# Attention and two MLPs on one core: an early first exponential, other decoding steps for the second MLP, state-row sums over 64 columns

## The chip, the core and the metric

The kernel runs on one core of a Trainium2 chip. The metric is the device time of one execution in microseconds (us); the median of several runs is compared. The engines have these names in profiles: PE (TensorE's matmuls), PEld (its weight loads, which overlap the matmuls), DVE (VectorE), ACT (ScalarE), POOL (GpSimd) and SP (SyncE, which issues most DMAs).

## What is computed

Cross attention between 8 x 8 heads' 512 tokens and 32 state rows, in both directions, then two MLPs over all 8 x (512 + 32) = 4352 rows of 512 features. All data are float32.

```python
scores = x @ state.T / sqrt(64)              # 512 x 32 per head
xread = softmax(scores) @ state              # 512 x 64
scores2 = state @ x.T / sqrt(64)             # 32 x 512
sread = softmax(scores2) @ x                 # 32 x 64: the state rows' sums over tokens
y = concat(xread, sread), heads side by side # (8 * 544) x 512
h = y @ w_in1;  g = h * sigmoid(1.702 * h);  y = g @ w_out1
h = y @ w_in2;  g = h * cos(h);              out = g @ w_out2
```

The inner width is 2048. The softmax subtracts the maximum and adds 1e-9 to the sum.

## The kernel before

**Tiles and steps.** Tokens are cut into nine tiles: t = 0 to 7 are the 512 tokens of one batch each, and t = 8 (the tail) holds all batches' 256 state rows, collected in `xs`. A step (m, t, c) handles MLP m, tile t and 128 of the 2048 inner columns, so a tile has 16 steps c. MLP 1 takes the tiles in the order 0 to 6, tail, 7; MLP 2 takes 0 to 3, tail, 4 to 7. In a step PE does `hidden` (the product with w_in, into `ph`), then `second` of two steps earlier (the product with w_out, added up in `py0` to `py3`, which have one buffer each). Between them lies the activation: `gate` in MLP 1 (tanh L383, multiply L385, high part gh L373, low part gl L375) and `cosine` in MLP 2 (L409 to L420, then `times`).

**Float32 in pieces.** Products are made of three passes of a rounded high part and a low part (`wh`, `wl`, `xh`, `xl`). Weights come packed as 64-bit words and are decoded on the chip, in sixteen units per MLP: eight of w_in and eight of w_out, 1 MB each. `fetch_w` loads a unit, `decode_begin` gives two ScalarE operations (`top` L121, `bottom` L124), and in the next step `decode_end` gives `bits` (VectorE, L137), `hi` (ScalarE, L143) and `lo` (VectorE, L147). `units` says in which step a unit is begun. The second MLP's units are begun at the steps of `at2` (L615), in the order w_in 0 to 7, w_out 0 to 7: four in the tail tile of MLP 1 (steps 6, 9, 12, 15), seven in tile 7 of MLP 1 (2, 4, ... 14) and five in the first tile of MLP 2 (3, 5, 7, 10, 12).

**Order.** The whole order is written by hand (`tc.manual_schedule`): each engine runs its instructions in the order in which the Python code issues them, and so does each queue. Loads of a step stand on SP's queue behind all earlier ones.

**Attention.** `attn_pieces(b, g)` gives the pieces for batch b and half g (four heads). `scores` multiplies four heads at a time, each in its own 32 columns of the array; q counts these heads. `max_n`, `exp_n`, `norm_n`, `xread` are the softmax over state rows and the product with the states; `max_s`, `exp_s`, `norm_s`, `turn_s`, `sread`, `place_s` are the softmax over tokens, a transpose, the sums over tokens and their transposes into `xs`. For batches 1 to 7 xread isn't formed: `sw_piece` multiplies states and w_in once, from `rhi` and `rlo`, the two parts of a pair of batches' states in `rblk`, and stores the products in DRAM; `load_sw` loads them. `split_state` makes rhi and rlo; `load_pair` loads the states of a pair.

In `sread` each of four heads multiplies its 32 weight columns with the 128 columns of its head pair, of which only 64 are its own; `place_s` picks those. There are sixteen such sums, each of four token chunks times four heads, and each matmul shows as two in the trace (two passes).

**The start.** Batch 0 is done before the first step. ScalarE's queue issues the loads of `sblk`, `rblk` and `pair0`, then makes rhi of `pair0`; then follow both halves' softmax, `warm(22)` (22 matmuls on the identity, into a place that nothing reads), `xread` and the decoding of the first unit.

**Output.** `store` copies py to `o` and issues the store. In MLP 2, `o` comes from a pool with two buffers.

```python
pool, tag = (ep, "g") if m == 0 and k >= 2 else (op, "o")
```

## Time and profile before

| | us |
|---|---|
| three runs | 1468.28, 1467.53, 1468.15 |
| their median | 1468.15 |
| the profiled execution | 1467.7 |
| its span, from the first to the last instruction | 1465.9 |
| PE busy | 1446.3 (99%) |
| PEld busy | 1188.5 (81%) |
| DVE busy | 928.1 (63%) |
| ACT busy | 646.9 (44%) |
| POOL busy | 112.9 (8%) |

Times in rows are counted from the start of the span. A matmul's busy time overlaps that of the next, so PE's pace is read from starts, not from durations. In a row of a timeline, the bracket gives how long the engine was idle just before, and what ended that; instructions of one line that follow one another are merged (x count). "L366" is line 366 of the kernel. Where an instruction waits for several things, the profile names the one that came last by its own records.

### The profile page before, as it was taken

The page shows a single profiled execution, that of the slowest core. Times are in us where ns is not written, and L with a number is a line of the kernel's source. Part 1 is how long each engine was busy: PE and PEld are TensorE (multiplying, and loading weights), DVE is VectorE, ACT ScalarE, POOL GpSimd, SP SyncE. Part 2 cuts the span into 40 slices and gives each one's busy share as a digit, 9 for nine tenths or more (in the row PEclk, how much of TensorE's full clock was granted, in tenths as well). Part 3 has the DMA queues.
Part 4 walks back from the last instruction along what each step waited for, and adds up shares of the span by engine and source line. Part 5 has one row for each costly group of instructions (what it writes and reads, how often), then busy time and mean ns, then how long its engine had stood idle before and what let it go on. Part 6 is the DMA issues. An engine that isn't in the chain of part 4 may idle for free.

```text
span 1465.9 us, 19331 instructions
## 1 busy us (share of the span) xinstructions
PE 1446.3 (99%) x7310; PEld 1188.5 (81%) x7310; DVE 928.1 (63%) x1641; ACT 646.9 (44%) x1078; POOL 112.9 (8%) x156
## 2 busy tenths in 40 slices
PE   8999999999999999999999999999999999999998
PEld 5878888888887888998877888888888888888886
DVE  6875655565555655456687666666677666666664
ACT  5864344434334343466555333333343343333433
POOL 0111011101010000100000010100000000101000
PEclk9999999999999999999999999999999999999999
DMA  9756565655655353564400101010011000010000
GB/s 341 224 178 195 140 187 140 177 158 144 175 133 166 99 145 108 180 191 169 144 1 0 58 1 58 1 44 0 1 59 44 1 32 26 0 58 1 29 1 29
DMA packets 81340, 140.58 MB, mean 96 GB/s; under 512 B 11616, under 2 KB 38368, under 8 KB 81248
## 3 DMA queue, kind: packets, MB, share of 16 engines
q1 hardware_dynamic: 70944, 109.34, 23.6%
q0 software_dynamic: 8960, 29.37, 8.1%
q8 instruction: 57, 0.93, 0.3%
q10 hardware_dynamic: 1344, 0.66, 0.2%
q14 instruction: 35, 0.29, 0.1%
HBM read 92.14 MB, written 47.19 MB: 95 GB/s over the span
## 4 chain that ended last, share of the span: by engine, by line
PE 88%; DVE 7%; ACT 3%; issue 1%; DMA 1%; POOL 0%; ACTq 0%; DVEq 0%
PE py L452 46%; PE ph L366 26%; PE ph L359 11%; PE psS L176 3%; PE psA L235 1%; PE psC L319 1%; DVE u L137 1%; DVE r L413 1%; DVE r L418 1%; DVE d L417 1%; DVE wo L147 1%; ACT wo L143 1%; PE psB L310 1%; DVE gl L375 1%; ACT rawo L124 0%
## 5 line engine op out<-in xcount | busy, mean ns | idle before, releaser
L366 PE MATMUL ph<-xh,wi 128*128 128x512 f32 (+1 forms) x1280 | 404.6, 379 | 0.0
L452 PE MATMUL py<-gh,wo 128*128 128x512 f32 (+1 forms) x1152 | 362.6, 378 | 2.4 <-ACT wo L143 1.2
L452 PE MATMUL py<-wo,gh 128*128 128x512 f32 x1088 | 335.5, 390 | 0.2 <-ACT gh L373 0.2
L366 PEld LDWEIGHTS ph<-xh,wi 128*128 128x128 f32 x1280 | 237.8, 188 | 49.2 <-DVE xl L287 1.3
L452 PEld LDWEIGHTS py<-gh,wo 128*128 128x128 f32 x1152 | 213.0, 188 | 44.7 <-DVE wo L147 2.0
L366 PE MATMUL ph<-xl,wi 128*128 128x512 f32 (+1 forms) x640 | 241.4, 379 | 0.0
L452 PEld LDWEIGHTS py<-wo,gh 128*128 128x128 f32 x1088 | 203.2, 188 | 41.5 <-ACT gh L373 0.7
L452 PE MATMUL py<-gl,wo 128*128 128x512 f32 (+1 forms) x576 | 217.4, 377 | 0.0
L452 PE MATMUL py<-wo,gl 128*128 128x512 f32 x544 | 212.9, 391 | 4.5 <-DVE gl L375 4.2
L420 ACT ACTIVATE r<-r,half_pi 128x512 f32<-128x512 f32 (+1 forms) x144 | 101.0, 701 | 245.7 <-DVE r L419 245.7
L375 DVE TENSOR_TENSOR gl<-t,gh 128x512 fp32r<-128x512 f32 (+1 forms) x144 | 97.4, 676 | 159.1 <-ACT gh L373 159.1
L373 ACT ACTIVATE gh<-t 128x512 fp32r<-128x512 f32 (+1 forms) x144 | 87.7, 609 | 248.1 <-PE py L452 137.1
L413 DVE TENSOR_SCALAR r<-r 128x512 f32<-128x512 f32 (+1 forms) x144 | 65.5, 455 | 182.4 <-ACT r L409 182.3
L359 PE MATMUL ph<-xh,swt 128*128 128x512 f32 x448 | 160.5, 399 | 0.0
L409 ACT ACTIVATE r<-ph 128x512 f32<-128x512 f32 (+1 forms) x144 | 82.3, 572 | 171.6 <-PE ph L366 171.5
L385 DVE SCALAR_TENSOR_TENSOR t<-t,ph 128x512 f32<-128x512 f32 (+1 forms) x144 | 94.1, 654 | 84.3 <-ACT t L383 84.1
L366 PEld LDWEIGHTS ph<-xl,wi 128*128 128x128 f32 x640 | 120.6, 188 | 22.7
L452 PEld LDWEIGHTS py<-wo,gl 128*128 128x128 f32 x544 | 102.0, 188 | 30.2 <-DVE gl L375 9.2
L452 PEld LDWEIGHTS py<-gl,wo 128*128 128x128 f32 x576 | 108.4, 188 | 20.1
L433 DVE TENSOR_TENSOR r<-r,ph 128x512 f32<-128x512 f32 (+1 forms) x144 | 94.8, 658 | 41.5 <-ACT r L420 41.4
L383 ACT ACTIVATE t<-ph 128x512 f32<-128x512 f32 (+1 forms) x144 | 82.0, 570 | 81.1 <-PE ph L359 65.0
L184 POOL DMA_DIRECT2D sd<-swo x112 | 67.0, 608 | 528.1 <-DVE swo L181 505.9
(78 smaller groups left out, 1505.6 us busy)
## 6 DMA issues: line engine op xcount, KB each, us to landing
sd<-swo POOLq DMA_DIRECT2D x112, 256.0 KB, 3.8
swt<-sd SPq DMA_DIRECT2D x112, 256.0 KB, 4.0
rawi<-in_w_in SPq DMA_DIRECT2D x32, 512.0 KB, 6.5
rawo<-in_w_out SPq DMA_DIRECT2D x32, 512.0 KB, 5.7
xT_t<-in_xT SPq DMA_DIRECT2D x36, 256.0 KB, 4.3
xN_t<-in_xN SPq DMA_DIRECT2D x16, 512.0 KB, 4.2
yd<-o SPq DMA_DIRECT2D x32, 256.0 KB, 2.9
yraw<-yd SPq DMA_DIRECT2D x32, 256.0 KB, 4.4
```

The lines of the kernel that those rows point to most:

```text
L184: nc.gpsimd.dma_start(out=sw_dram[b, f][r0:r0 + D, :, k // 2, :], in_=o[i * D:(i + 1) * D].bitcast(F32).rearrange("p c h f -> p c (h f)"))
L359: nc.tensor.matmul(ph, l, r, start=(g == 0 and i == 0), stop=(g == 1 and i == 2))
L366: nc.tensor.matmul(ph, w[:, f0:f0 + P], x, start=(w is wh and k == 0 and x is xk[0][0]), stop=(w is wl and k == KD - 1))
L373: nc.scalar.activation(out=gh, in_=g, func=AF.Copy)
L375: return lambda: nc.vector.tensor_tensor(out=gl, in0=g, in1=gh.bitcast(F32), op=ALU.subtract)
L383: nc.scalar.activation(out=t1, in_=ph, func=AF.Tanh, scale=0.5 * GATE)
L385: nc.vector.scalar_tensor_tensor(out=g, in0=t1, scalar=1.0, in1=ph, op0=ALU.add, op1=ALU.mult)
L409: nc.scalar.activation(out=r, in_=ph, func=AF.Copy, scale=1.0 / (2.0 * math.pi), bias=0.25)
L413: nc.vector.tensor_scalar(out=r, in0=r, scalar1=MAGIC, scalar2=MAGIC, op0=ALU.add, op1=ALU.subtract)
L420: nc.scalar.activation(out=r, in_=r, func=AF.Sin, bias=half_pi)
L433: nc.vector.tensor_tensor(out=r, in0=r, in1=ph, op=ALU.mult)
L452: nc.tensor.matmul(yt[k], l, r, start=(c == 0 and i == 0), stop=(c == KF - 1 and i == 2))
```

## The change

It has four parts.

1. At the start the first ScalarE instruction is now an exponential of one column (`early`). `pair0` is gone: pair 0 is loaded into `rblk` where pair 1 was, `rhi` and `rlo` of pair 0 are made at step 1 of tile 0 (rlo by POOL), and pair 1 is loaded three steps later. The load of `rblk` moves from ScalarE's queue to SP's. `max_n` is cut into `lay_n` and `most_n`, the pieces of the two halves change their order, and `warm(22)` becomes `warm(16)` before the first xread and `warm(14)` behind it.
2. The second MLP's units are begun at other steps: five in the tail of MLP 1 (6, 8, 10, 12, 14), eight in tile 7 (0, 2, ... 14), three in the first tile of MLP 2 (4, 7, 10).
3. `sread` multiplies each head's weights with its own 64 columns, and `place_s` reads columns 0 to 63.
4. In MLP 2 the third and fourth output copy of a tile go to the tiles aT and a2T, which have one buffer each and are not used by attention any more there.

```diff
--- before.py
+++ after.py
@@ -203,16 +203,16 @@
     def load_state(b, queue=nc.sync):
         queue.dma_start(out=rblk.rearrange("p k d -> p (k d)"), in_=st[b])
 
-    def load_pair(p, into=rblk, queue=nc.sync):
+    def load_pair(p):
 
         for i in range(2):
-            queue.dma_start(
-                out=into[:, :, i * D:(i + 1) * D], in_=stT[(*PAIRS[p], 0)[i]].rearrange("p (k c) -> p k c", k=KD)
+            nc.sync.dma_start(
+                out=rblk[:, :, i * D:(i + 1) * D], in_=stT[(*PAIRS[p], 0)[i]].rearrange("p (k c) -> p k c", k=KD)
             )
 
-    def split_state(src=rblk, engine=nc.vector):
-        nc.scalar.activation(out=rhi, in_=src, func=AF.Copy)
-        engine.tensor_tensor(out=rlo, in0=src, in1=rhi.bitcast(F32), op=ALU.subtract)
+    def split_state(engine):
+        nc.scalar.activation(out=rhi, in_=rblk, func=AF.Copy)
+        engine.tensor_tensor(out=rlo, in0=rblk, in1=rhi.bitcast(F32), op=ALU.subtract)
 
     def load_xT(b, g, tags=("xT0", "xT1")):
         for j in range(2):
@@ -239,8 +239,14 @@
 
 
         def max_n():
+            lay_n()
+            most_n()
+
+        def lay_n():
             v["T"] = at.tile([P, S // NS, NS], F32, name="T", tag=at_T)
             nc.vector.transpose(out=v["T"].rearrange("p a n -> p (a n)"), in_=v["A"])
+
+        def most_n():
             v["m1"] = sm.tile([P, S // NS], F32, name="m1", tag="m1")
             nc.vector.tensor_reduce(out=v["m1"], in_=v["T"], axis=AX.X, op=ALU.max)
 
@@ -280,8 +286,8 @@
                 v["X", j] = ps_x[j][0].tile([P, S], F32, name="psX", tag=ps_x[j][1])
                 nc.tensor.matmul(v["X", j], rblk[a, 2 * g + j, :], v["aT"][a, :], start=True, stop=True)
 
-        def split_x():
-            for j in range(2):
+        def split_x(js=range(2)):
+            for j in js:
                 hi, lo = xtile["x", b][2 * g + j]
                 nc.scalar.activation(out=hi, in_=v["X", j], func=AF.Copy)
                 nc.vector.tensor_tensor(out=lo, in0=v["X", j], in1=hi.bitcast(F32), op=ALU.subtract)
@@ -317,8 +323,8 @@
             for c in range(n):
                 for q in range(4):
                     nc.tensor.matmul(
-                        v["C"][q * NS:(q + 1) * NS, :P], v["a2T"][:, c * P + q * NS:c * P + (q + 1) * NS],
-                        ld[b, g, "n"][:, c, (q // 2) * P:(q // 2 + 1) * P],
+                        v["C"][q * NS:(q + 1) * NS, :D], v["a2T"][:, c * P + q * NS:c * P + (q + 1) * NS],
+                        ld[b, g, "n"][:, c, q * D:(q + 1) * D],
                         start=(c == 0), stop=(c == n - 1),
                     )
 
@@ -329,11 +335,11 @@
                     p0 = (h % 2) * D + 32 * e
                     nc.vector.transpose(
                         out=xs[p0:p0 + 32, h // 2, b * NS:(b + 1) * NS],
-                        in_=v["C"][32 * q:32 * q + 32, p0:p0 + 32],
+                        in_=v["C"][32 * q:32 * q + 32, 32 * e:32 * e + 32],
                     )
 
         return dict(
-            scores=scores, max_n=max_n, exp_n=exp_n, norm_n=norm_n, sum_n=sum_n, turn_n=turn_n, high_n=high_n,
+            scores=scores, max_n=max_n, lay_n=lay_n, most_n=most_n, exp_n=exp_n, norm_n=norm_n, sum_n=sum_n, turn_n=turn_n, high_n=high_n,
             low_n=low_n, xread=xread, split_x=split_x, max_s=max_s, exp_s=exp_s, norm_s=norm_s, turn_s=turn_s,
             sread=sread, place_s=place_s,
         )
@@ -454,7 +460,7 @@
 
     def store(m, t, k):
         n = sizes[t]
-        pool, tag = (ep, "g") if m == 0 and k >= 2 else (op, "o")
+        pool, tag = (op, "o") if k < 2 else (ep, "g") if m == 0 else (at, ("aT", "a2T")[k - 2])
         o = pool.tile([P, n if m == 0 else DM], F32, name="o", tag=tag)
         nc.scalar.activation(out=o, in_=yt[k], func=AF.Copy, scale=0.5 if m == 0 else 1.0)
         if m == 0:
@@ -559,12 +565,11 @@
         load_xT(0, 0)
         load_state_t(0, nc.scalar)
         load_xT(0, 1, ("a20", "a21"))
-        load_state(0, nc.scalar)
-        pair0 = at.tile([P, KD, P], F32, name="pair0", tag="xN")
-        load_pair(0, pair0, nc.scalar)
+        load_state(0)
         fetch_w(0, *seq[0])
         make_identity(nc, ident)
         nc.vector.memset(half_pi, math.pi / 2.0)
+        nc.scalar.activation(out=sm.tile([P, 1], F32, name="early", tag="b2"), in_=half_pi, func=AF.Exp)
         first = [
             attn_pieces(0, 0, ((ps_h, "ph"), (ps_h, "ph"))),
             attn_pieces(0, 1, ((ps_y, "py0"), (ps_y, "py1")), "a2T", "a21"),
@@ -583,21 +588,23 @@
             for name in names:
                 first[int(name[-1])][name[:-2]]()
 
-        split_state(pair0, nc.gpsimd)
-        do("max_n 0", "exp_n 0")
+        do("max_n 0", "exp_n 0", "lay_n 1")
         for part in decode_begin(0, *seq[0]):
             part()
-        do("max_n 1", "exp_n 1", "sum_n 0", "turn_n 0")
-        warm(22)
+        do("sum_n 0", "turn_n 0")
+        warm(16)
         load_xN(1, 0)
-        do("xread 0")
+        do("xread 0", "most_n 1")
+        warm(14)
         bits, hi, lo = decode_end()
         bits()
+        first[0]["split_x"]((0,))
+        do("exp_n 1")
         hi()
-        do("sum_n 1", "turn_n 1", "split_x 0")
+        do("sum_n 1", "turn_n 1", "xread 1")
+        first[0]["split_x"]((1,))
         lo()
-        do("xread 1")
-        load_pair(1)
+        load_pair(0)
         for part in decode_begin(0, *seq[1]):
             part()
         do("split_x 1")
@@ -612,7 +619,7 @@
         units = {(0, 0, c): (0, *u) for c, u in enumerate(seq[2:])}
         fetches.update({steps1[steps1.index((0, B, 0)) + 2 * j + 2]: (1, "i", j) for j in range(KF // 2)})
         fetches.update({steps[steps.index((0, B - 1, 0)) + 2 * j + 3]: (1, "o", j) for j in range(KF // 2)})
-        at2 = [(0, B, c) for c in (6, 9, 12, 15)] + [(0, B - 1, c) for c in range(2, KF, 2)] + [(1, 0, c) for c in (3, 5, 7, 10, 12)]
+        at2 = [(0, B, c) for c in range(6, KF, 2)] + [(0, B - 1, c) for c in range(0, KF, 2)] + [(1, 0, c) for c in (4, 7, 10)]
         units.update({at_: (1, nm, j) for at_, (nm, j) in zip(at2, ((nm, j) for nm in "io" for j in range(KF // 2)))})
         for i, (m, t, c) in enumerate(steps):
             if m == 0 and c == 0 and t + 1 < B:
@@ -630,9 +637,9 @@
                 lo = cosine(t, c, stores, steps[i - 1][1:] if steps[i - 1][0] == 1 else None, unit, i + 1 == len(steps))
             if (m, t, c) in fetches:
                 fetch_w(*fetches[m, t, c])
-            if m == 0 and todo_split.get((t, c), 0):
-                split_state()
-            if m == 0 and todo_split.get((t, c - 3), 0) and todo_split[t, c - 3] + 1 < len(PAIRS):
+            if m == 0 and (t, c) in todo_split:
+                split_state(nc.vector if t else nc.gpsimd)
+            if m == 0 and (t, c - 3) in todo_split and todo_split[t, c - 3] + 1 < len(PAIRS):
                 load_pair(todo_split[t, c - 3] + 1)
             for b, name in todo.pop(i, ()):
                 run_piece(b, int(name[-1]), name[:-2])
```

Parts 1 and 2 move instructions. On ACT, the start of the program, before (`T` are the scores of a half, `u` and `rawi` belong to the first unit, `xh` to xread):

```order
L201 DMA sblk<-in_stT 128x256
L204 DMA rblk<-in_st 128x512
L209 DMA pair_146<-in_stT 128x4x64 x2
L214 ACT_TABLE_LOAD
L214 ACTIVATE rhi<-pair_146 128x512
L250 ACTIVATE T<-T 128x512
L121 ACTIVATE u<-rawi_0_149 128x1024
L124 ACTIVATE rawi_0_149<-rawi_0_149 128x1024
L250 ACTIVATE T<-T 128x512
L143 ACTIVATE wi_0_253<-u 128x1024
L286 ACTIVATE xh_157<-psX 128x512
L286 ACTIVATE xh_159<-psX 128x512
```

And now:

```order
L201 DMA sblk<-in_stT 128x256
L572 ACT_TABLE_LOAD
L572 ACTIVATE early<-half_pi 128x1
L256 ACTIVATE T<-T 128x512
L121 ACTIVATE u<-rawi_0_146 128x1024
L124 ACTIVATE rawi_0_146<-rawi_0_146 128x1024
L292 ACTIVATE xh_156<-psX 128x512
L256 ACTIVATE T<-T 128x512
L143 ACTIVATE wi_0_261<-u 128x1024
L292 ACTIVATE xh_158<-psX 128x512
L121 ACTIVATE u<-rawi_1_180 128x1024
L124 ACTIVATE rawi_1_180<-rawi_1_180 128x1024
```

The loads of `rblk` and `pair`, and rhi, have left the front; the first xh stands before the second half's exponential.

On DVE, from behind the second half's first transpose on, before (`m` are maxima, `s` sums, `r` reciprocals, `xl` the low parts of xread):

```order
L245 TENSOR_REDUCE m_211<-T 128x16
L259 TENSOR_REDUCE s_215<-T 128x16
L260 TENSOR_SCALAR s_215<-s_215 128x16
L262 RECIPROCAL r_218<-s_215 128x16
L263 TENSOR_TENSOR T<-T,r_218 128x512
L267 STREAM_TRANSPOSE aT<-T 128x512
L137 SCALAR_TENSOR_TENSOR u<-u,rawi_0_149 128x1024
L259 TENSOR_REDUCE s_255<-T 128x16
L260 TENSOR_SCALAR s_255<-s_255 128x16
L262 RECIPROCAL r_258<-s_255 128x16
L263 TENSOR_TENSOR T<-T,r_258 128x512
L267 STREAM_TRANSPOSE aT<-T 128x512
```

And now:

```order
L265 TENSOR_REDUCE s_208<-T 128x16
L266 TENSOR_SCALAR s_208<-s_208 128x16
L268 RECIPROCAL r_211<-s_208 128x16
L269 TENSOR_TENSOR T<-T,r_211 128x512
L273 STREAM_TRANSPOSE aT<-T 128x512
L251 TENSOR_REDUCE m_239<-T 128x16
L137 SCALAR_TENSOR_TENSOR u<-u,rawi_0_146 128x1024
L293 TENSOR_TENSOR xl_157<-psX,xh_156 128x512
L265 TENSOR_REDUCE s_263<-T 128x16
L266 TENSOR_SCALAR s_263<-s_263 128x16
L268 RECIPROCAL r_266<-s_263 128x16
L269 TENSOR_TENSOR T<-T,r_266 128x512
```

The second half's maximum has moved from before the first half's sum to behind its transpose `aT`, and one subtraction `xl` stands before the second half's sum.

On ACT, from the end of MLP 1's tail tile into tile 7, before (128x256 rows are the tail's, 128x512 tile 7's, `o` the tail's output copies):

```order
L124 ACTIVATE rawi_3_5923<-rawi_3_5923 128x1024
L383 ACTIVATE t_6195<-ph 128x512
L373 ACTIVATE gh<-t_6195 128x512
L143 ACTIVATE wi_3_6202<-u 128x1024
L383 ACTIVATE t_6230<-ph 128x512
L459 ACTIVATE o<-py_5670 128x256
L373 ACTIVATE gh<-t_6230 128x512
L459 ACTIVATE o<-py_5671 128x256
L459 ACTIVATE o<-py_5672 128x256
L459 ACTIVATE o<-py_5673 128x256
L383 ACTIVATE t_6275<-ph 128x512
```

And now:

```order
L143 ACTIVATE wi_4_6193<-u 128x1024
L389 ACTIVATE t_6217<-ph 128x512
L121 ACTIVATE u<-rawi_5_6084 128x1024
L379 ACTIVATE gh<-t_6217 128x512
L124 ACTIVATE rawi_5_6084<-rawi_5_6084 128x1024
L389 ACTIVATE t_6250<-ph 128x512
L465 ACTIVATE o<-py_5680 128x256
L379 ACTIVATE gh<-t_6250 128x512
L465 ACTIVATE o<-py_5681 128x256
L465 ACTIVATE o<-py_5682 128x256
L465 ACTIVATE o<-py_5683 128x256
L143 ACTIVATE wi_5_6269<-u 128x1024
```

Unit 5 is now begun in the first step of tile 7, and its `wi_5` stands behind the four output copies of the next step.

## Rows read from the trace of the kernel before

**Rows 1.** Page, part 1: busy time, share and instructions of each engine.
```profile
PE 1446.3 (99%) x7310; PEld 1188.5 (81%) x7310; DVE 928.1 (63%) x1641; ACT 646.9 (44%) x1078; POOL 112.9 (8%) x156
```
**Rows 2.** Chain of waits, end of the kernel: start us, us, what.
```profile
1443.65 5.44 PE ph L366 x24
```
**Rows 3.** Windows, PE alone: stretch, us, PE busy (x), granted clock, DMA share, GB/s.
```profile
19.40:21.50 2.10, 2.10 (x7) 0.50 1.09 377
```
**Rows 4.** Timeline, 9 to 24 us: start us, us, engine line op tiles [idle before <-releaser].
```profile
9.29 0.63 ACT L214 ACTIVATE rhi<-pair 128x512 fp32r<-128x512 f32 x1
9.82 0.61 ACT L250 ACTIVATE T<-T 128x512 f32<-128x512 f32 x1
...
14.13 1.13 PE L281 MATMUL psX<-aT,rblk 64*128 64x512 f32 x4 [0.36 <-DVE aT L267]
...
17.80 1.72 PE L281 MATMUL psX<-aT,rblk 64*128 64x512 f32 x4 [2.54 <-DVE aT L267]
...
19.45 0.79 PE L366 MATMUL ph<-xh,wi 128*128 128x512 f32 x1
...
23.49 0.60 ACT L383 ACTIVATE t<-ph 128x512 f32<-128x512 f32 x1 [2.86 <-PE ph L366]
```
**Rows 5.** Timeline of ACT, first tile of the second MLP: its first step and the next tile's.
```profile
708.50 0.60 ACT L409 ACTIVATE r<-ph 128x512 f32<-128x512 f32 x1 [1.14 <-PE ph L366]
...
799.84 0.60 ACT L409 ACTIVATE r<-ph 128x512 f32<-128x512 f32 x1 [1.53 <-PE ph L366]
```
**Rows 6.** Timeline, 1068 to 1072 us, ACT and PE.
```profile
1068.06 0.60 ACT L459 ACTIVATE o<-py 128x512 f32<-128x512 f32 x1 [2.22 <-PE ph L366]
...
1071.78 0.50 PE L452 MATMUL py<-wo,gl 128*128 128x512 f32 x1 [0.49 <-DVE gl L375]
```
**Rows 7.** Timeline, the kernel's end, PE and ACT.
```profile
1460.40 0.39 PE L452 MATMUL py<-wo,gl 128*128 128x512 f32 x1
...
1461.50 1.34 ACT L459 ACTIVATE o<-py 128x512 f32<-128x512 f32 x2 [1.45 <-DMA out<-o]
```
**Rows 8.** Timeline of PE, 73.3 to 75.6 us: a row sum and the scores behind it.
```profile
73.66 1.08 PE L319 MATMUL psC<-xN_t,a2T 128*32 128x128 f32 x32
74.56 1.04 PE L235 MATMUL psA<-xT_t,sblk 128*32 128x512 f32 x8
75.53 0.50 PE L366 MATMUL ph<-xh,wi 128*128 128x512 f32 x1
```
**Rows 9.** Timeline of the first 0.05 us of that row sum, PE and PEld.
```profile
73.66 0.32 PE L319 MATMUL psC<-xN_t,a2T 128*32 128x128 f32 x4
...
73.66 0.16 PEld L319 LDWEIGHTS psC<-xN_t,a2T 128*32 128x32 f32 x8 [0.35 <-issue]
```
**Rows 10.** Timeline of ACT, MLP 1's tail tile, around one unit's decoding.
```profile
626.63 0.39 ACT L383 ACTIVATE t<-ph 128x256 f32<-128x256 f32 x1
...
628.70 1.06 ACT L143 ACTIVATE wi<-u 128x1024 fp32r<-128x1024 f32 x1 [0.27 <-DVE u L137]
...
631.44 0.42 ACT L373 ACTIVATE gh<-t 128x256 fp32r<-128x256 f32 x1 [1.41 <-DVE t L385]
632.39 0.39 ACT L383 ACTIVATE t<-ph 128x256 f32<-128x256 f32 x1 [0.53 <-PE ph L366]
...
633.77 0.42 ACT L373 ACTIVATE gh<-t 128x256 fp32r<-128x256 f32 x1
...
635.27 0.39 ACT L383 ACTIVATE t<-ph 128x256 f32<-128x256 f32 x1
```
**Rows 11.** Timeline of PE, first py of tile 7.
```profile
650.37 0.50 PE L452 MATMUL py<-gh,wo 128*128 128x512 f32 x1 [0.29 <-ACT o L459]
```
**Rows 12.** Windows: us, PE, PEld, DVE, ACT, POOL busy (x), granted clock, DMA share, GB/s.
```profile
708.00:800.00 92.00, 89.21 (x389) 72.22 (x388) 69.66 (x106) 49.51 (x72) 6.22 (x4) 1.00 0.12 43
800.00:1064.00 264.00, 264.00 (x1178) 219.07 (x1177) 171.57 (x294) 100.86 (x172) 13.22 (x12) 1.00 0.07 23
```
**Rows 13.** Page, part 6: line engine op xcount, KB each, us to landing.
```profile
rawo<-in_w_out SPq DMA_DIRECT2D x32, 512.0 KB, 5.7
```

## The prediction

> **What bounds the kernel now.** The profile's page comes first: TensorE is busy 99% of the span [rows 1]. Its matmuls follow one another at a fixed pace, 24 of 512 columns in 5.44 us, 0.227 us each, as the chain of waits shows for a whole stretch on PE [rows 2]. So time can only come from fewer streamed columns on PE, from places where PE waits, and from the two ends. The windows and timelines show four such places. At the start nothing of the MLPs runs before 19.45 us, and PE's clock is at 0.50 (1.2 of 2.4 GHz) from about there to 21.5 us, after 2.54 us in which PE waited for a transpose of VectorE, the second aT [rows 3, 4]. At the first tile of the second MLP sixteen steps take 799.84 - 708.50 = 91.34 us instead of 16 x 5.44 = 87.04: 4.3 us lost [rows 2, 5]. At 1068 us ScalarE waits 2.22 us with an output copy and PE then idles 0.49 us [rows 6]. At the end ScalarE waits 1.45 us for a store to land before the last two copies [rows 7].
>
> **The start.** Removed ahead of the first exponential on ScalarE: the wait for `pair0`, and rhi, 0.63 us right before its start at 9.82 [rows 4]. The table load moves to where ScalarE has nothing to do. Also gone from the front: 256 KB of `pair0` loads; the `rblk` load now stands on SP behind the four xT loads. Both let data arrive a little earlier. Against this VectorE now does the reduction of group 1 and one more subtraction (xl) between the two aT transposes. So the second aT, there at 17.80, comes anywhere from 1.2 us sooner to 0.5 us later; I take 0.5 sooner. What matters more is that 14 filling matmuls and the first xread now stand ahead of it, so that PE does not idle 2.5 us there. An xread of this kind took 1.13 us at 14.13 and 1.72 us at 17.80 [rows 4]: 0.6 less. The first twelve MLP matmuls took 23.49 - 19.45 = 4.04 us, partly at half clock; at 0.227 us and 0.3 for the first load and the drain they take 3.0: 1.0 less [rows 2, 4]. Together **-2.1** (0 to -2.6). rhi and rlo are not gone: they now stand at step 1 of tile 0, where ScalarE has a unit to decode in every step. 0.63 us of ScalarE [rows 4] is the upper bound, zero the lower, if the step's slack takes it; I take **+0.5**. rlo goes to POOL, idle there; pair loads on SP come where pair 1 stood, and the next one behind a weight load that is used much later. I cost these at nothing; if SP were late, the first table of products would wait, not PE's main line.
>
> **The row sums (sread).** Sixteen sums, each 32 matmul passes, four tiles of 32 columns of the array at a time, so eight steps. They start at 73.66 and the scores behind them at 74.56: 0.90 us, 0.112 a step [rows 8]. The scores use the same tiles with 512 columns, 8 passes in two steps, and what follows starts at 75.53: 0.485 us a step at most [rows 8]. Four times the columns cost 4.3 times the step, so there is next to nothing fixed in it, and 64 columns should take half of 0.112: 0.056 x 8 = 0.45 us less for a sum. I take 0.42, since a change of tiles has some fixed part, 6.8 us for sixteen. That is an extension below the smallest size that the trace has, so its bounds are -6.8 and 0 (steps that do not shrink). Two of the sums lie in tile 0, where other engines also hold PE up; I count them half: **-6.4**. The loads of 32 weights don't stand in its way as far as the row goes: eight of them begin within 0.06 us [rows 9]. The DVE transposes keep their number and size.
>
> The Trainium skill has a rule against this gain. Its page "TensorE: Matmul & The Clock Gate" (section "Wait — 56ns, not 53.3ns?") says that starts of matmuls never come closer than about 25 ns, however few the columns. By it 32 starts take 0.8 us and one sum saves 0.1 us at most, the whole 1.5 us instead of 6.8. The rows here are mixed on this: the mean distance, 0.90 us over 32, is 28 ns, but four starts lie within the first 0.05 us [rows 9], so starts in different tiles do come closer; I follow the latter.
>
> **Second MLP's decoding: the tail tile of MLP 1.** Units of w_in now begin every second step there instead of every third. PE sets their pace with 24 passes of 256 columns, 2.88 us a step (635.27 - 632.39) [rows 10]. A unit's chain alternates ScalarE and VectorE. From a tanh to the unit's `hi` 628.70 - 626.63 = 2.07 us; from `hi` to the gh of the next step 631.44 - 628.70 = 2.74; from a gh over the second ScalarE operation of a unit to the next tanh 635.27 - 633.77 = 1.50: 6.31 us for two steps that PE does in 5.76 [rows 10]. With three steps the 0.55 us are made up; with two they add up over four intervals to 2.2 us and with the 512-wide step after them to some 3 us. The gate's lead of two steps on PE covers it until tile 7's first steps, where py must be freed by the tail's four output copies; those stand behind these tanhs. PE waited for them there already, until 650.37 [rows 11]; the lead covers part of the 3 us, and I take nearer the upper end, since the copies are what PE stops at: **+1.8** (0 to +3). From there on steps are longer than the chain, and nothing builds up.
>
> **First tile of MLP 2.** Five units become three, three steps apart. VectorE is at 69.66 of 92 us there against 171.57 of 264 where no unit runs, 0.65 [rows 12]; that leaves 1.9 us a step, and a unit takes (69.66 - 0.65 x 92) / 4 = 2.5 us (four to five units lie in the window). Every third step the spare 5.7 us take that with ease, every second step 3.8 us hardly. Of the 4.3 us, three fifths (2.6) would stay if loss went by units alone, none if spacing decides; two of the three units still meet the splits of y at steps 7 to 11. I leave 1.4: **-2.9** (-1.7 to -4.3). The two w_out units that move into tile 7 take places that w_in units had, so they cost nothing there; their loads are issued three steps ahead, over 8.6 us, and land after 5.7 [rows 13].
>
> **Output copies.** In MLP 2 the third and fourth copy get buffers of their own. At 1068 the profile names PE for the 2.22 us wait of ScalarE; I read it as the wait for an earlier store, as the row of the end has it. It goes and with it PE's 0.49 and the refill after it: **-0.7** (0 to -0.8) [rows 6]. For the other full tiles, with steps twice as long on PE, I count nothing. At the end, PE is done at 1460.79, and the copies end at 1461.50 + 1.34 = 1462.84; without the wait the last ends 0.62 after PE, at 1461.41: **-1.4** (-1.2 to -1.5) [rows 7]; the landing after it stays.
>
> Sum: -2.1 + 0.5 - 6.4 + 1.8 - 2.9 - 0.7 - 1.4 = -11.2 us. The profiled execution took 1467.7 us (span 1465.9 and 1.8 around it), so 1456.5; the median of the runs, 1468.15, lies 0.45 above it: **1457.0 us**.
>
> **Rivals.** (B) The steps of sread stay at 0.11 us, since each of the 32 matmuls has a start distance of 28 ns that fewer columns don't shorten: 6.4 us come back, 1463.4. For it: that mean distance, and that no row has fewer than 128 columns. Against: from 128 to 512 columns the step grows as the columns do, and four starts lie together. By the Trainium skill's 25 ns (same page and section) it would be 1463.4 - 1.4 = 1462.0, an estimate; its chance is in that of (B). (C) The tail's chain costs far more than the stop at py: the w_in units delay each other on into tile 7, +5 instead of +1.8: 1460.2. For it: 6.31 against 5.76. Against: steps of tile 7 are longer, and units of the same number ran there every second step without a wait of PE. (D) Slower: before, two tiles of a step read the same 128 columns; now all four read different ones. If PE feeds different columns one tile after another, a step takes 4 x 0.056 = 0.224 us instead of 0.112; 128 steps cost 14.3 us more, where I counted 6.4 less: 1477.7. It turns slower than before once a step takes more than about 0.15 us, as all other terms give 4.8. Against: the two different ranges of scores run side by side. (E) The table load, the fills or the order at the start don't do what they are for: PE's clock still falls before the first MLP matmuls, 1459; inside my range.
>
> **Chances.** Forecast with (E) 0.66, (B) 0.18, (C) 0.08, (D) 0.04, the rest spread. The forecast's own range, with its bounds, is 1453 to 1460.5; taking in (B) it goes to 1463.5. A measurement of this kernel tells 0.2% (2.9 us) from no change. All but (D) and a pile of bad bounds lie below 1465.2: faster 0.93, same 0.03, slower 0.04.
>
> **What would show it.** The start of a row sum and of the scores behind it some 0.48 us apart; 0.90 again means (B), more means (D). The first MLP matmul near 18.3 us with the clock at 1.00, first tanh near 21.3. A longer stop of PE at the first py of tile 7 than that before 650.37, with the copies late. MLP 2's first tile below 89 us for sixteen steps. No wait of ScalarE for a store in MLP 2, and the span's end 1.4 us sooner after the last matmul. I am wrong if sread does not shrink, or if PE waits in tile 7 for more than 3 us.

## The result and the profile after

| | before | after |
|---|---|---|
| median of the runs, us | 1468.22 | 1455.49 |
| lowest to highest | 1467.53 to 1468.62 | 1454.74 to 1455.64 |
| the profiled execution | 1467.7 | 1455.64 |
| its span | 1465.9 | 1453.8 |

The ratio of after to before is 0.9908, with a 95% interval of 0.9896 to 0.9919. The forecast was 1457.0, with a range of 1453.0 to 1463.5.

The rows below answer to those of before. First the page's busy times [rows 1]. TensorE is still at 99%, now with 1438.6 us of work.

```profile
PE 1438.6 (99%) x7326; PEld 1184.2 (81%) x7326; DVE 926.4 (64%) x1641; ACT 647.2 (45%) x1079; POOL 112.2 (8%) x156
```

The timeline of the start [rows 4] (start us, us, engine, line, operation, tiles, in brackets the idle time before and its releaser):

```profile
2.47 0.20 ACT L572 ACTIVATE early<-half_pi 128x1 f32<-128x1 f32 x1
...
9.19 0.63 ACT L256 ACTIVATE T<-T 128x512 f32<-128x512 f32 x1 [6.52 <-DVE T L255]
...
12.09 1.16 ACT L121 ACTIVATE u<-rawi 128x1024 f32<-128x1024 f32 x1 [2.26 <-DMA rawi<-in_w_in]
...
14.31 1.24 DVE L137 SCALAR_TENSOR_TENSOR u<-u,rawi 128x1024 int32<-128x1024 int32 x1 [1.12 <-ACT rawi L124]
...
15.46 0.70 DVE L293 TENSOR_TENSOR xl<-psX,xh 128x512 fp32r<-128x512 f32 x1
...
18.77 1.13 PE L287 MATMUL psX<-aT,rblk 64*128 64x512 f32 x4 [1.29 <-DVE aT L273]
...
19.83 0.50 PE L372 MATMUL ph<-xh,wi 128*128 128x512 f32 x1
...
22.93 0.60 ACT L389 ACTIVATE t<-ph 128x512 f32<-128x512 f32 x1 [1.91 <-PE ph L372]
```

The first exponential is 0.6 us sooner, and the second xread takes 1.13 us at the full clock instead of 1.72. But it starts 0.97 us *later*, at 18.77 instead of 17.80. The first tanh comes only 0.56 us sooner.

The timeline of DVE shows the two transposes `aT` that the two xreads wait for, before and then after:

```profile
13.37 0.71 DVE L267 STREAM_TRANSPOSE aT<-T 128x512 f32<-128x512 f32 x1
...
17.04 0.71 DVE L267 STREAM_TRANSPOSE aT<-T 128x512 f32<-128x512 f32 x1
```

```profile
11.92 0.71 DVE L273 STREAM_TRANSPOSE aT<-T 128x512 f32<-128x512 f32 x1
...
18.00 0.71 DVE L273 STREAM_TRANSPOSE aT<-T 128x512 f32<-128x512 f32 x1
```

The first now comes 1.45 us sooner, but the second starts 6.08 us behind it instead of 3.67.

The timeline of PE at the first row sum [rows 8]:

```profile
73.10 0.66 PE L325 MATMUL psC<-xN_t,a2T 128*32 128x64 f32 x32
73.57 1.04 PE L235 MATMUL psA<-xT_t,sblk 128*32 128x512 f32 x8
```

From the start of the sum to the scores behind it 0.47 us, where it was 0.90.

The timeline of ACT and PE at the first py of tile 7 [rows 11]. PE stops twice there, for output copies that come late:

```profile
642.18 0.37 ACT L465 ACTIVATE o<-py 128x256 f32<-128x256 f32 x1
...
642.60 0.50 PE L458 MATMUL py<-gh,wo 128*128 128x512 f32 x1 [0.77 <-ACT o L465]
...
643.62 0.91 ACT L465 ACTIVATE o<-py 128x256 f32<-128x256 f32 x3
644.04 0.50 PE L458 MATMUL py<-gh,wo 128*128 128x512 f32 x1 [0.48 <-ACT o L465]
```

A bracket counts the idle time from the modelled end of the matmul before. Against the pace of 0.227 us from start to start, the two stops cost 0.93 and 0.65 us, and the matmul behind each a further 0.11, so 1.8 us together. Such stops "with refills" are meant below. The one stop of before cost 0.56.

The timeline of ACT in the tail shows why the copies come late. These are the tanhs behind the `hi` of two units that follow each other:

```profile
625.77 0.36 ACT L389 ACTIVATE t<-ph 128x256 f32<-128x256 f32 x1
...
631.93 0.36 ACT L389 ACTIVATE t<-ph 128x256 f32<-128x256 f32 x1
```

They lie 6.16 us apart, as do all such neighbours from 613.45 to 638.09 us, where PE's pace for two steps is 5.76. So ScalarE falls 0.4 us further behind with each unit.

The timeline at the first tile of MLP 2 [rows 5], its first step and the next tile's, and the one stop of PE that is left in it:

```profile
702.18 0.60 ACT L415 ACTIVATE r<-ph 128x512 f32<-128x512 f32 x1 [1.14 <-PE ph L372]
...
773.73 0.50 PE L458 MATMUL py<-wo,gl 128*128 128x512 f32 x1 [0.36 <-DVE gl L381]
...
789.93 0.60 ACT L415 ACTIVATE r<-ph 128x512 f32<-128x512 f32 x1 [1.71 <-PE ph L372]
```

Sixteen steps take 87.75 us instead of 91.34.

The timeline of ACT in MLP 2's tail tile [rows 6], then of PE and ACT at the end [rows 7]:

```profile
1054.64 1.97 ACT L465 ACTIVATE o<-py 128x512 f32<-128x512 f32 x3
...
1056.90 0.59 ACT L465 ACTIVATE o<-py 128x512 f32<-128x512 f32 x1
...
1448.08 2.68 ACT L465 ACTIVATE o<-py 128x512 f32<-128x512 f32 x4 [1.31 <-PE py L458]
...
1449.73 0.39 PE L458 MATMUL py<-wo,gl 128*128 128x512 f32 x1
```

No copy waits for a store. The last one ends at 1448.08 + 2.68 = 1450.76, 0.64 us behind PE's last matmul, where it was 2.05.

The two traces laid over each other at the first operation of ScalarE in each tile tell where the 12.1 us between the spans lie:

| stretch | forecast | measured |
|---|---|---|
| to the first tanh | -2.1 | -0.56 |
| rhi and rlo in step 1 | +0.5 | 0.0 |
| from there to the tail tile (sixteen row sums) | -6.4 | -7.0 |
| tail tile and first py of tile 7 | +1.8 | +1.26 |
| first tile of MLP 2 | -2.9 | -3.59 |
| MLP 2's tail tile | -0.7 | -0.76 |
| after the last matmul | -1.4 | -1.41 |
| sum | -11.2 | -12.1 |

### The profile page after: what moved, and what is told of

Its sections match the earlier page's. It is cut to its first block, busy times and chain, and to the rows that moved or that the text cites. A ratio compares the mean times of both kernels' runs of the same rounds, so it can differ in the third digit from the quotient of the medians.

```text
span 1453.8 us, 19362 instructions
## 1 busy us (share of the span) xinstructions
PE 1438.6 (99%) x7326; PEld 1184.2 (81%) x7326; DVE 926.4 (64%) x1641; ACT 647.2 (45%) x1079; POOL 112.2 (8%) x156
## 4 chain that ended last, share of the span: by engine, by line
PE 91%; DVE 4%; ACT 2%; DMA 1%; issue 1%; SPq 0%; POOL 0%; ACTq 0%; DVEq 0%
PE py L458 48%; PE ph L372 27%; PE ph L365 11%; PE psS L176 3%; DMA rawi<-in_w_in 1%; PE psA L235 1%; DVE u L137 1%; PE psC L325 1%; PE psB L316 1%; ACT wi L143 1%; DVE wi L147 1%; DVE r L419 0%; ACT rawi L124 0%; DVE wo L147 0%; DVE t L391 0%
## 5 line engine op out<-in xcount | busy, mean ns | idle before, releaser
L391 DVE SCALAR_TENSOR_TENSOR t<-t,ph 128x512 f32<-128x512 f32 (+1 forms) x144 | 94.0, 653 | 75.9 <-ACT t L389 75.6
L365 PEld LDWEIGHTS ph<-xh,swt 128*128 128x128 f32 x448 | 84.4, 188 | 27.8 <-issue 10.9
```

Of the source, the lines that this page charges most:

```text
L365: nc.tensor.matmul(ph, l, r, start=(g == 0 and i == 0), stop=(g == 1 and i == 2))
L391: nc.vector.scalar_tensor_tensor(out=g, in0=t1, scalar=1.0, in1=ph, op0=ALU.add, op1=ALU.mult)
```

## The experiments

The theory is the table above: parts that lie in different stretches and add up. The rivals are told with each experiment. Where a part is priced, the traces are compared stretch by stretch. Medians of the same kernel differ from one group of runs to another: the changed kernel had 1455.49 us first and 1456.71 later, and the kernel before lay between 1467.75 and 1469.50.

**The row sums over 128 columns again** (`wide_sums`: the changed kernel with this part undone).

```diff
-    v["C"][q * NS:(q + 1) * NS, :D], ...
-    ld[b, g, "n"][:, c, q * D:(q + 1) * D],
+    v["C"][q * NS:(q + 1) * NS, :P], ...
+    ld[b, g, "n"][:, c, (q // 2) * P:(q // 2 + 1) * P],
```

> The changed kernel with one part undone: the row sums over 128 columns again. Theory (a step of four tiles costs by its columns, nothing else hangs on it): from the first start of a sum to the scores behind it 0.90 us again instead of 0.47, sixteen times 0.43: 6.8 us more, 1462.3 us. Rival (part of the gain came from the start or from a stop of PE that moved): the sums in the trace take 0.90 us again, but the time rises by less than 5 us, below 1460.5, because PE then waits less elsewhere.

Measured: 1461.87 us (0.995 of before, 0.9937 to 0.9962). The timeline of PE at the first sum:

```profile
72.44 1.08 PE L325 MATMUL psC<-xN_t,a2T 128*32 128x128 f32 x32
73.34 1.04 PE L235 MATMUL psA<-xT_t,sblk 128*32 128x512 f32 x8
```

0.90 us again. Between the first tanh and the tail tile this kernel loses 6.85 us to the changed one (its start was 0.69 us sooner). PE stops no less elsewhere, so the theory holds and the rival falls.

**Half of each row sum** (`narrow_sums`), the disputed cost once more at a smaller size.

```diff
-    v["C"][q * NS:(q + 1) * NS, :D], ...
-    ld[b, g, "n"][:, c, q * D:(q + 1) * D],
+    v["C"][q * NS:(q + 1) * NS, :NS], ...
+    ld[b, g, "n"][:, c, q * D:q * D + NS],
```

> The changed kernel with only 32 of each head's 64 columns multiplied in the row sums, so half of each sum is left out. Theory (a step of four tiles costs by its columns alone, 0.056 us for 64): a sum takes about 0.24 us from its first start to the scores behind it instead of 0.47; sixteen times 0.22 is 3.6 us less, 1451.9 us. Rival (32 matmul starts have a shortest time of their own, and 0.47 us is already near it): a sum stays at 0.40 to 0.47 us and the time at 1454.5 to 1455.5.

Measured: 1452.79 us (ratio 0.9893, 0.9876 to 0.9911). The timeline of PE at the first sum:

```profile
73.25 0.46 PE L325 MATMUL psC<-xN_t,a2T 128*32 128x32 f32 x32
73.52 1.08 PE L235 MATMUL psA<-xT_t,sblk 128*32 128x512 f32 x8
```

0.27 us, where 0.24 was expected and the rival wanted 0.40 or more. With 0.90, 0.47 and 0.27 for 128, 64 and 32 columns a sum has a small fixed part of some 0.05 us, and the rest goes with the columns. From the first tanh to the tail the sixteen sums save another 2.65 us, less than sixteen times 0.20 and less than the 3.6 expected: behind eight of the sums stand scores, and these now take 1.02 us to the next product instead of 0.97, so a quarter of the gain is lost there.

**The old decoding steps** (`old_steps`).

```diff
-        at2 = [(0, B, c) for c in range(6, KF, 2)] + [(0, B - 1, c) for c in range(0, KF, 2)] + [(1, 0, c) for c in (4, 7, 10)]
+        at2 = [(0, B, c) for c in (6, 9, 12, 15)] + [(0, B - 1, c) for c in range(2, KF, 2)] + [(1, 0, c) for c in (3, 5, 7, 10, 12)]
```

> The changed kernel with the old decoding steps of the second MLP. Theory (spacing decides both stretches): PE's two stops at the first py of tile 7 (about 1.8 us with the refills behind them) shrink to the one of before, about 0.55; the first tile of MLP 2 loses about 4.2 us again instead of 0.6. Net 2.3 more: 1457.8 us. Rival (the stop at py belongs to the other parts of the change, not to the spacing in the tail): the stops stay at 1.8 us and the time is 1459.1.

Measured: 1457.45 us (ratio 0.992, 0.9908 to 0.9932). The timeline of PE, the stop at tile 7's first py and the two longest in the first tile of MLP 2:

```profile
642.89 0.50 PE L458 MATMUL py<-gh,wo 128*128 128x512 f32 x1 [0.29 <-ACT o L465]
...
757.88 0.50 PE L458 MATMUL py<-wo,gl 128*128 128x512 f32 x1 [1.26 <-DVE gl L381]
...
787.00 0.50 PE L458 MATMUL py<-wo,gl 128*128 128x512 f32 x1 [0.95 <-DVE gl L381]
```

Only the one short stop at tile 7 is left, 1.2 us won there, and in the first tile of MLP 2 five stops lose 3.55 us to the changed kernel: net 2.4, where 2.3 was expected. The stop at py does belong to the decoding steps. In this trace the tanhs behind the `hi` of neighbouring units in the tail lie 8.64 us apart, three steps of PE's pace, so with three steps ScalarE doesn't fall behind.

**Two buffers for all copies of MLP 2** (`old_store`).

```diff
-        pool, tag = (op, "o") if k < 2 else (ep, "g") if m == 0 else (at, ("aT", "a2T")[k - 2])
+        pool, tag = (ep, "g") if m == 0 and k >= 2 else (op, "o")
```

> The changed kernel with two buffers for all output copies of MLP 2. Theory (ScalarE's 2.2 us wait near 1060 us was for the landing of an earlier store): PE stops about 0.6 to 0.8 us once more at the tail tile of MLP 2, and the last two copies end 2.0 us after the last matmul instead of 0.6: together 2.1 more, 1457.6 us. Rival (that wait was for PE, as the profile names it): only the end comes back, 1.4 more, 1456.9, and there is no stop near 1060 us.

Measured: 1456.37 us (ratio 0.9913, 0.9899 to 0.9926). The timeline of ACT, tail tile of MLP 2 and end:

```profile
1056.94 0.60 ACT L465 ACTIVATE o<-py 128x512 f32<-128x512 f32 x1 [1.49 <-DMA out<-o]
...
1450.40 1.26 ACT L465 ACTIVATE o<-py 128x512 f32<-128x512 f32 x2 [1.50 <-DMA out<-o]
```

Half and half. The wait is for a store, as the theory has it. But it is 1.49 us long, not 2.22, and PE doesn't stop behind it: the first store landed 2.1 us after its issue, against 2.8 in the trace of before. So only the 1.4 us of the end came back, as the rival said, though for another reason than the rival's.

**The old start** (`old_start`: the kernel before with the 64-column sums, the new decoding steps and the new output buffers).

```diff
--- before.py
+++ old_start
+                        v["C"][q * NS:(q + 1) * NS, :D], ...
...
+        pool, tag = (op, "o") if k < 2 else (ep, "g") if m == 0 else (at, ("aT", "a2T")[k - 2])
...
+        at2 = [(0, B, c) for c in range(6, KF, 2)] + [(0, B - 1, c) for c in range(0, KF, 2)] + [(1, 0, c) for c in (4, 7, 10)]
```

> The kernel before with the 64-column sums, the new decoding steps and the new output buffers, that is the changed kernel with the old start. Theory (the change at the start moved the second aT back by as much as the full clock gave): PE's clock falls to 0.50 at the first MLP matmuls again and the first tanh starts at 23.5 instead of 22.9 us, 0.6 more: 1456.1 us. Rival (the start gave what the prediction counted, 2.1 less 0.5, and the difference is hidden in other stretches): 1.6 more, 1457.1 us.

Measured: 1455.72 us (ratio 0.9912, 0.9898 to 0.9925). The timeline of PE at the second xread, then the windows of PE (stretch, us, PE busy, granted clock, DMA share, GB/s):

```profile
18.04 1.13 PE L281 MATMUL psX<-aT,rblk 64*128 64x512 f32 x4 [2.43 <-DVE aT L267]
```

```profile
18.00:19.40 1.40, 1.36 (x5) 1.00 1.09 351
19.40:21.50 2.10, 2.07 (x9) 1.00 1.09 375
```

Neither. With the same instructions as before up to the first step, PE idled 2.43 us ahead of the second xread, about as before, and its clock stayed at 1.00. The first tanh came at 22.53, sooner than in the changed kernel's own trace. One trace of a start does not price it.

**The kernel before, once more** (`before_again`), for a second trace of it.

> The kernel before once more, for a second trace of its start and of its tail tile of MLP 2. Theory (the half clock before 21.5 us and PE's stop near 1071 us in the first trace depend on when loads and stores land in an execution): at least one of the two is missing here or stands elsewhere; where the first store of the tile lands within 2.1 us of its issue there is no stop near 1071, and the first tanh is at 22.5 us where the clock stays at 1.00, at 23.5 where it doesn't. Rival (both belong to the kernel): clock 0.50 from about 18 to 21.5 us, first tanh at 23.5, and PE idle about 0.5 us near 1071 us.

Measured: 1469.09 us beside 1467.77 for the other runs of the same kernel (1.001, 0.9998 to 1.0022). The windows of PE, then the timeline of ACT and PE in MLP 2's tail tile:

```profile
19.40:21.50 2.10, 2.10 (x6) 0.50 1.09 377
32.00:36.00 4.00, 3.47 (x10) 0.60 1.09 366
```

```profile
1069.68 0.60 ACT L459 ACTIVATE o<-py 128x512 f32<-128x512 f32 x1 [2.50 <-DMA out<-o]
...
1073.39 0.50 PE L452 MATMUL py<-wo,gl 128*128 128x512 f32 x1 [0.76 <-DVE gl L375]
```

Here the rival is right: half clock (1.2 GHz) in the first MLP matmuls again, first tanh at 23.37, and the stop in the tail tile is even longer, 0.76, behind a store that took 3.1 us. The second xread started before the clock fell and took 1.13 us. The half clock shows in two of three traces of the old start, and in none of the eight traces with the new start. A second stretch below full clock, at 33 to 36 us, is there in this trace and in two of those eight.

**Other decoding steps** (`later_steps`), three apart in the tail.

```diff
+        at2 = [(0, B, c) for c in (5, 8, 11, 14)] + [(0, B - 1, c) for c in range(1, KF, 2)] + [(1, 0, c) for c in (1, 5, 9, 13)]
```

> The changed kernel with the second MLP's units begun at steps 5, 8, 11, 14 of the tail, at the odd steps 1 to 15 of tile 7 and at 1, 5, 9, 13 of the first tile of MLP 2. Theory (a spacing of three steps keeps the tail's chain in time; in MLP 2 a unit costs a stop only where the step that ends it also has a split of y on GpSimd, at 7, 9, 11, 13, and here none does): the two stops at tile 7's first py (1.8 us with refills) shrink to 0.3 or less and the one of 0.6 in MLP 2's first tile goes: 1.7 to 2.2 less, 1453.5 us. Rival (in MLP 2 it is the number of units that costs): four units bring two or three stops, 1 to 2 us, and the time is 1454.5 to 1455.5.

Measured: 1454.54 us (ratio 0.9903, 0.9887 to 0.9919). The timeline of PE, first tile of MLP 2, then the windows of PE in tile 0:

```profile
724.77 0.50 PE L458 MATMUL py<-wo,gl 128*128 128x512 f32 x1 [0.77 <-DVE gl L381]
```

```profile
32.00:36.00 4.00, 3.73 (x10) 0.60 1.08 380
```

The median lies where the rival put it, but not for the rival's reason. Both stops at tile 7 are gone (1.8 us won there). In MLP 2's first tile units at 5, 9 and 13 cost nothing, but the one at step 1 brought a stop of 1.04 with its refill; the theory had missed it. By the traces the steps win 1.4 us. The span hides it, as this execution lost 1.6 us to the low clock of the window above.

**The low parts of y by VectorE** (`y_on_dve`).

```diff
-    split_y(order[j + 1], (c - 7) // 2, nc.gpsimd if m else nc.vector)
+    split_y(order[j + 1], (c - 7) // 2, nc.vector)
```

> The changed kernel with the low parts of y in MLP 2 made by VectorE instead of GpSimd. Theory (VectorE's first rounding of a step is held up while GpSimd works: 1.22 us instead of 0.29 in the tail tile of MLP 2, and PE's four stops there, 2.3 us with refills, come from that; on VectorE the subtraction takes 0.69): the stops at 1078 to 1097 us go, 2.3 less, and the rounding takes 0.29 us in every step: 1453.2 us. Rival (VectorE is short of time in that tile, whoever does the subtraction): the four stops stay at 1.5 us or more together, and the time is 1454.7 or above.

Measured: 1454.03 us (ratio 0.9902, 0.9887 to 0.9917). The timelines of POOL and DVE in MLP 2's tail tile, first of the changed kernel, then of this one:

```profile
1081.60 1.30 POOL L497 TENSOR_TENSOR xl<-yraw,xh 128x512 fp32r<-128x512 f32 x1 [4.98 <-ACT xh L496]
...
1081.82 1.22 DVE L419 TENSOR_SCALAR r<-r 128x256 f32<-128x256 f32 x1 [0.37 <-ACT r L415]
```

```profile
1082.37 0.69 DVE L497 TENSOR_TENSOR xl<-yraw,xh 128x512 fp32r<-128x512 f32 x1 [0.77 <-ACT xh L496]
...
1083.31 0.29 DVE L419 TENSOR_SCALAR r<-r 128x256 f32<-128x256 f32 x1
```

The rounding takes 0.29 us again in every step, as the theory says. The stops shrink from 2.3 to 1.3 us and don't go: 0.69 us on VectorE itself is shorter than the 0.93 of the hold-up, but more than the step has left. The gain is 1.0 in this stretch, between the two forecasts.

**The start once more** (`start_dve`).

```diff
+        fetch_w(0, *seq[0])
+        load_state(0)
...
+        spare = nc.vector
...
-        do("xread 0", "most_n 1")
+        do("xread 0", "most_n 1", "exp_n 1")
...
-        do("sum_n 1", "turn_n 1", "xread 1")
-        first[0]["split_x"]((1,))
+        do("sum_n 1", "turn_n 1", "xread 1", "low_x 0")
```

> The changed kernel with three changes at the start: the state rows' load stands behind the first unit's loads; the second half's subtraction of the maxima is VectorE's instead of GpSimd's; both low parts of the first xread stand behind the second aT. Theory (the second aT decides when the first MLP matmul starts, and it waits for the first unit's load, for a decoding step that is stretched beside GpSimd, and for a low part ahead of it): the first tanh starts at 21.2 to 21.7 us instead of 22.2 to 22.9; 1.0 less, 1454.5 us. Rival (the arrival of the loads sets it, and the order of VectorE doesn't matter): first tanh at 22.2 or later, 1455.5 us.

Measured: 1454.25 us (ratio 0.9905, 0.989 to 0.992). The timeline of DVE and PE in this kernel, then of POOL and DVE in `wide_sums`, whose start is that of the changed kernel:

```profile
12.69 0.69 DVE L255 TENSOR_TENSOR T<-T,m 128x512 f32<-128x512 f32 x1
...
13.30 1.22 DVE L137 SCALAR_TENSOR_TENSOR u<-u,rawi 128x1024 int32<-128x1024 int32 x1
...
17.14 1.13 PE L287 MATMUL psX<-aT,rblk 64*128 64x512 f32 x4 [0.55 <-DVE aT L273]
```

```profile
12.76 1.05 POOL L255 TENSOR_TENSOR T<-T,m 128x512 f32<-128x512 f32 x1 [11.45 <-DVE m L251]
12.84 2.05 DVE L137 SCALAR_TENSOR_TENSOR u<-u,rawi 128x1024 int32<-128x1024 int32 x1 [0.22 <-ACT rawi L124]
```

The second xread starts at 17.14, where the eight traces with the changed kernel's start have 18.06 to 18.90, and the first tanh at 21.65; the two combined kernels below have the same start and the first tanh at 21.71 and 21.73. The theory holds for the three edits together; they were not tried one by one. The same operation took 2.05 us beside GpSimd's subtraction and 1.22 without it.

The other way round shows in `narrow_sums`, also with the changed kernel's start, where `bits` began first. The timeline of DVE and POOL:

```profile
13.37 1.21 DVE L137 SCALAR_TENSOR_TENSOR u<-u,rawi 128x1024 int32<-128x1024 int32 x1
...
13.59 1.90 POOL L255 TENSOR_TENSOR T<-T,m 128x512 f32<-128x512 f32 x1 [12.28 <-DVE m L251]
```

Here `bits` took 1.21 us and GpSimd's subtraction 1.90 instead of 1.05.

**The changed kernel again and two combined kernels**, measured side by side. `combined` has the start of `start_dve`, other steps for the units, and the low parts of y in two halves on VectorE:

```diff
+        at2 = [(0, B, c) for c in (5, 8, 11, 14)] + [(0, B - 1, c) for c in (1, 3, 5, 7, 9, 11, 13, 14)] + [(1, 0, c) for c in (3, 6, 9, 13)]
...
-                if c in (7, 9, 11, 13):
-                    split_y(order[j + 1], (c - 7) // 2, nc.gpsimd if m else nc.vector)
+                if 7 <= c < 15:
+                    split_y(order[j + 1], (c - 7) // 2, (c - 7) % 2)
```

`combined_fill` adds `warm(4)` ahead of the first `second` of tile 0.

> The changed kernel once more, beside the two that follow. Theory (its parts are as worked out; what differs from run to run is when the first loads land and whether PE's clock falls once in the first 36 us): 1455.5 us, the first tanh between 22.2 and 23.0. Rival (the first result was a lucky one): above 1457.

> The changed kernel with the start of the experiment on the start, units at steps 5, 8, 11, 14 of the tail, 1, 3, 5, 7, 9, 11, 13, 14 of tile 7 and 3, 6, 9, 13 of the first tile of MLP 2, and the low parts of y made by VectorE in two halves, one in each of two steps. Theory (the gains lie in different stretches and add up): start 1.0, tile 7's first py 1.8, first tile of MLP 2 0.6, its tail tile 2.0 (half a subtraction, 0.35 us, fits into what VectorE has left in a step there): 5.4 less, 1450.1 us. Rival (VectorE has no room for the halves, and units three steps apart in MLP 2's first tile cost a stop beside them): 1.0 instead of 2.0 in the tail tile and 0.6 to 1.2 lost in the first: 1452 us.

> The combined kernel with four more filling matmuls (8 passes, 0.96 us) ahead of the first product with w_out in tile 0, where PE otherwise waits 1.3 us and where its clock stood at 0.50 for about 3.5 us in two of the nine profiles (1.5 us lost). Theory (that idle time is what the clock falls after): no stretch of the first 40 us below 1.00 behind the start, the best runs as those of the combined kernel and the slow ones nearer to them: median 0.3 to 0.5 less. Rival (the fills stand in the way of the product, or the clock falls all the same): the same spread, or 0.3 more.

| | median | lowest to highest | ratio to before |
|---|---|---|---|
| changed kernel | 1456.71 | 1454.28 to 1458.18 | 0.9919 (0.9903 to 0.9934) |
| combined | 1450.14 | 1449.75 to 1451.54 | 0.9877 (0.9863 to 0.989) |
| combined_fill | 1450.20 | 1449.43 to 1450.26 | 0.9874 (0.9861 to 0.9888) |

The changed kernel's second median lies 1.2 us above the first, between the two expectations; its runs spread over 3.9 us. `combined` is faster than both kernels. Its spans by stretch, against `after_again`: first tanh 0.5 sooner, tail and tile 7 1.8, first tile of MLP 2 0.3, tail tile of MLP 2 2.1, together 4.7 us, where 5.4 was expected. The trace of `after_again` has an early start; against the first trace of the changed kernel the last matmul comes 5.4 us sooner. The timeline of DVE in that tail tile shows the half of a low part:

```profile
1083.49 0.43 DVE L502 TENSOR_TENSOR xl<-yraw,xh 128x256 fp32r<-128x256 f32 x1 [0.76 <-ACT xh L501]
```

The fill keeps PE at work in tile 0, as the timeline of PE in `combined_fill` shows:

```profile
28.60 1.05 PE L508 MATMUL idle<-ident 128*128 128x128 f32 x8
29.91 0.50 PE L461 MATMUL py<-gh,wo 128*128 128x512 f32 x1 [0.26 <-ACT wo L143]
```

Its median is no lower. Its four runs lie closer together than the four without the fill, but the difference there is one run. Whether the fill keeps the clock up stays open.

## Why the prediction was right, point by point

**Row sums: right, and a little more.** The step of four tiles went from 0.112 to 0.059 us (0.47 us over eight steps), where 0.056 was worked out. `wide_sums` and `narrow_sums` show that the columns set nearly all of it. The two sums in tile 0 gave their full share too, where I had counted them half: 16 x 0.43 = 6.8 of the 7.0 us in that stretch. Rival (B), a start distance that doesn't shrink, and rival (D), four different ranges of columns fed one after another, both fall by the one row [rows 8] and its answer: 32 starts in 0.47 us are 14.7 ns each, and in `narrow_sums` 0.27 over 32 is 8.4. The Trainium skill's rule of about 25 ns between starts (page "TensorE: Matmul & The Clock Gate", section "Wait — 56ns, not 53.3ns?") differs from that measurement, and the measurement decides: it doesn't hold for matmuls that go to different column tiles in turn.

**The start: the wrong size, by one step.** The forecast of -2.1 was 0.5 for an earlier second aT, 0.6 for the second xread and 1.0 for the first twelve MLP matmuls. Against the first trace of before, the last two came as worked out: from xread to the first MLP matmul 1.06 us instead of 1.65, from there to the tanh 3.10 instead of 4.04. The step that failed is "I take 0.5 sooner": the second aT came 0.97 later, outside that step's own bounds. The wait for `pair0` and rhi did go, as the first aT shows, but the distance from the first aT to the second grew by 2.4 us. The reduction (0.64) and the low part (0.70) that the prediction had listed are 1.3 of this. The other 1.1 are, in this trace, the wait of VectorE's `bits` for ScalarE, which waited 2.26 us for the first unit's load. "Both let data arrive a little earlier" is not borne out for this load: it now stands behind the state rows' on the same queue, and ScalarE could begin with it between 10.33 and 12.13 us in the eight traces with this start, against 10.99 to 11.75 in the three with the old one.

Yet the late load is not the whole cause, for the distance between the two transposes is 5.96 to 6.08 us in all eight. In three of them (`after`, `old_steps`, `later_steps`) `bits` waits for the load. In three (`after_again`, `wide_sums`, `old_store`) the load comes more than 1 us sooner, but `bits` takes 1.8 to 2.05 us beside GpSimd's subtraction. In two (`narrow_sums`, `y_on_dve`) `bits` is done early, but the subtraction beside it takes 1.90 us, and the second half's exponential waits for that. `start_dve` undoes all of this together: its distance is 4.99, and its second xread starts 0.9 to 1.8 us sooner. Which share each edit has was not tried.

The gain is also less fixed than one trace makes it look: the eight traces of the new start have their first tanh at 22.2 to 23.1 us, mean 22.60, the three of the old one at 23.49, 22.53 and 23.37, mean 23.13. The 0.6 and the 1.0 are won only against an old start that lost its clock; where it kept the clock (22.53, `old_start`), the new start gains nothing by its mean. Rival (E), a clock that still falls before the first MLP matmuls, is seen in none of the eight.

**rhi: nothing instead of +0.5.** From the first tanh to the end of PE's first stop in tile 0 the traces take 8.17 us and, before, 8.18, and the stop costs 1.30 us against PE's pace instead of 1.32. The step's slack took it, the lower bound.

**Tail of MLP 1: right in kind, +1.26 instead of +1.8.** The chain ran late and the copies held PE up, as the prediction had it: two steps of it took 6.16 us, where 6.31 was worked out, against PE's 5.76. `old_steps` and `later_steps`, with three steps between units, have no such stop or only the short one of before; they also begin tile 7's first unit later, and that share was not tried alone. Rival (C) fell: nothing built up in tile 7. I had set the forecast as what comes on top and taken it near the upper end; the two stops cost 1.8 in all, but 0.56 of that was there before.

**First tile of MLP 2: -3.59 instead of -2.9.** Of the 1.4 us that I left in place only 0.6 stayed. The three fifths by number of units are the wrong half of that estimate: spacing did more. But spacing is not all: one unit at step 1 cost 1.0 us in `later_steps`, and units at 5, 9, 13 nothing.

**Output copies: right at the end, right by luck at 1071 us.** The end gave 1.41. The stop at 1071 went, 0.76, but `old_store` has two buffers and no stop; its store landed in 2.1 us, and in the two traces of before it took 2.8 and 3.1. The term is the price of late landings, not of the two buffers alone. It is not one store: in the three tiles ahead, too, ScalarE waits 2.2 to 2.7 us for a store in both traces of before, and 1.7 in `old_store`. What makes stores land late there was not tried.

So the sum, -11.2 against -12.1, was close partly because errors of both signs met: 1.5 too much at the start, and 0.5, 0.6, 0.5 and 0.7 too little elsewhere. The forecast's own range without rival (B), 1453 to 1460.5, is narrower than its bounds added up with the sums at -6.4 or better, 1452.2 to 1462.5.

## What to carry to other kernels

Price an edit from a step whose size changes with it in rows you have (0.112 us a step at 128 columns, four times that at 512), and check a rule on single matmuls against a row where tiles run side by side. At a start that waits for loads, one trace is a sample: ask how the arrival times and the clock of another execution would change each term, above all where the gain is read from a stretch at half clock. Before work goes to an idle engine, look whether the busy one runs longer beside it; here the subtraction in two halves on the busy engine was cheaper than the whole on the idle one.

## What the runs showed of the hardware

Two VectorE operations that read and write SBUF alone took longer beside a subtraction of GpSimd, by about the time that they lay beside it: the rounding 1.22 us instead of 0.29 while GpSimd was at work from 1081.60 to 1082.90, `bits` 2.05 instead of 1.22 at the start. The Trainium skill (page "SBUF — State Buffer", section "SBUF: two separate sides") says that the two engines share a pair of ports, which the one that starts first holds for a whole instruction while the other, in some of VectorE's operations, waits. The traces agree in kind: where GpSimd began first, `bits` was the longer one (1.82 to 2.05 us, three traces), and where `bits` began first, GpSimd's subtraction was (1.90 instead of 1.05, two traces). They don't show the whole rule, as the rounding ended 0.14 us after the subtraction, less than its own 0.29, and GpSimd's spans in the profile are rough. In MLP 2's tail tile PE lost 2.3 us in four stops beside these subtractions, which the prediction had left as they were; with the halves on VectorE 2.1 of it went.

PE's clock fell to 0.50 (1.2 of 2.4 GHz) after much the same idle time in some executions and not in others: after 2.54 us in both traces of before, not after 2.43 in `old_start`; and behind the waits of tile 0 near 31 us (1.3 and 0.7 us against PE's pace) in three of thirteen traces without the fill, at about 1.6 us each time.
